# The opening layer norm split anew between ScalarE and VectorE, and sixteen one-column products moved ahead of the first q matmul

## The chip, the cores and the metric

One core of one Trainium2 chip. The metric is device time in microseconds (us) of one execution. "PE" is TensorE's matmuls, "PEld" its weight loads, "DVE" VectorE, "ACT" ScalarE, "POOL" GpSimd, "SP" the engine that issues nearly all DMAs. Executions of the same program on the same chip spread by about 1 us here (0.1%), which is more than the whole effect that this change aims at. A load "lands" when its last packet has arrived; a "slot" is the time from the start of one matmul to the start of the next.

## The reference, cut to what matters

```python
mod = silu(c) @ w_mod                  # six vectors of 1024: shift sa, scale ca, ...
h   = layernorm(x) * (1 + ca) + sa     # x: 2048 x 1024
x   = x + ga * linear_attention(h, wqkv, wo)      # q = h @ wqkv[:, :1024], ...
h   = layernorm(x) * (1 + cb) + sb
x   = x + gb * (silu(h @ w_gate) * (h @ w_up)) @ w_down
```

Only the first norm of the first 512 rows (row tiles 0 to 3), the scale `ca`, the shift `sa` and the first q matmuls matter here.

Of the kernel before, what the change touches and what calls it, by code (L numbers as in the profile page):

```python
# [8 lines left out]
ACT = mybir.ActivationFunctionType  # L9
ALU = mybir.AluOpType  # L10
# [252 lines left out]
def bass_adaLN_cond__linear_attn_block__swiglu_ffn__prompt_kernel(  # L263
# [20 lines left out]
    EPS = 1e-5  # L284

    with ExitStack() as es:
# [14 lines left out]
        XRES = T("xres", 0, [128, NST, D], BF16)  # L301
        PQT = T("pqt", 32 * KB, [128, NHG, S], BF16)
        WCA = T("wca", 32 * KB, [128, NDT, D], BF16)
# [12 lines left out]
        MV = T("mv", SM + 1632, [128, NST, 2], FP32)  # L316
        VE = T("ve", SM + 1760, [128, NST], FP32)
        RSTD = T("rstd", SM + 1824, [128, NST], FP32)
        NEGHALF = T("neghalf", SM + 1888, [128, 4], FP32)
        SUMX = T("sumx", SM + 1920, [128, NST], FP32)  # L320
        SUMSQ = T("sumsq", SM + 1984, [128, NST], FP32)
# [11 lines left out]
        NMR = T("nmr", SM + 2944, [128, NST], FP32)  # L333
# [119 lines left out]
        def warm(n=1, bank=2):  # L453
            for _ in range(n):
                P.pe("matmul", out=PS[:, bank, :], lhsT=IDENT[:], rhs=E1[:, 0, :], start=True, stop=True)
# [6 lines left out]
        def ln1_stats_ops(st):  # L462
            par, j = (st // 4) % 2, st % 4
            return [
                lambda: P.dve("bn_stats", out=STATS[:, par, j, 0, :], in_=XRES[:, st, 0:512]),
                lambda: P.dve("bn_stats", out=STATS[:, par, j, 1, :], in_=XRES[:, st, 512:1024]),
                lambda: P.dve("bn_aggr", out=MV[:, st, :], in_=STATS[:, par, j, :, :]),
            ]
# [10 lines left out]
        def ln1_xn(st):  # L479
            P.dve("tensor_scalar", out=XRES[:, st, :], in0=XRES[:, st, :],  # L480
                  scalar1=MV[:, st, 0:1], scalar2=RSTD[:, st:st + 1], op0=ALU.subtract, op1=ALU.mult)
# [22 lines left out]
        def mod_sc(w, c0, ms):  # L504
            for m in ms:
                for kt in range(NDT):
                    P.pe("matmul", out=PS[:, 0, c0 + m:c0 + m + 1], lhsT=w[:, kt, m * 128:(m + 1) * 128],
                         rhs=SILUC[:, kt:kt + 1], start=mod_first[0], stop=(kt == NDT - 1), skip_group_check=True)
                    mod_first[0] = False
# [48 lines left out]
        def ln1_rstd1(st):  # L558
            P.dve("tensor_scalar", out=VE[:, st:st + 1], in0=MV[:, st, 1:2], scalar1=EPS, scalar2=None, op0=ALU.add)
            P.pool("tensor_tensor", out=RSTD[:, st:st + 1], in0=VE[:, st:st + 1], in1=NEGHALF[:, 0:1], op=ALU.pow)  # L560

        def ln1_xn_act(st):
            P.dve("tensor_scalar", out=NMR[:, st:st + 1], in0=MV[:, st, 0:1], scalar1=RSTD[:, st:st + 1],
                  scalar2=-1.0, op0=ALU.mult, op1=ALU.mult)
            P.act("activation", out=XRES[:, st, :], in_=XRES[:, st, :],
                  func=ACT.Identity, scale=RSTD[:, st:st + 1], bias=NMR[:, st:st + 1])
# [7 lines left out]
        def act_stats(st, c0=0, mid=None):  # L574
            n = (D - c0) // 512
            junk0 = HT[:, 1, 0:2, :] if st < 8 else JUNK1
            for fn_, sc_, acc_ in ((ACT.Identity, 1.0 / D, SUMX), (ACT.Square, D ** -0.5, SUMSQ)):
                P.act("activation", out=junk0[:, 0:n, :], in_=XRES[:, st, c0:D].rearrange("p (a b) -> p a b", a=n),
                      func=fn_, scale=sc_, accum_out=acc_[:, st:st + 1])
                if mid is not None:  # L580
                    mid()
                    mid = None

        def act_mv_ops(st):
            return [
                lambda: P.dve("tensor_copy", out=MV[:, st, 0:1], in_=SUMX[:, st:st + 1]),
                lambda: P.dve("scalar_tensor_tensor", out=MV[:, st, 1:2], in0=SUMX[:, st:st + 1],
                              scalar=SUMX[:, st:st + 1], in1=SUMSQ[:, st:st + 1], op0=ALU.mult, op1=ALU.subtract),
            ]

        def neg_rstd(st):
            P.dve("tensor_scalar", out=VE[:, st:st + 1], in0=MV[:, st, 1:2], scalar1=-1.0, scalar2=EPS, op0=ALU.mult,
                  op1=ALU.add)
            P.pool("tensor_tensor", out=RSTD[:, st:st + 1], in0=VE[:, st:st + 1], in1=NEGHALF[:, 0:1], op=ALU.pow)

        act_stats(2)
        s0_, s1_, s3_ = ln1_stats_ops(0), ln1_stats_ops(1), ln1_stats_ops(3)
        m2 = act_mv_ops(2)

        def tile_transposes(*js):  # L600
            for dt in range(NDT):
                for j in js:
                    c = (dt % 2) * 512 + j * 128
                    P.pe("transpose", out=PSB[:, 4 + dt // 2, c:c + 128], in_=XRES[:, j, dt * 128:(dt + 1) * 128],
                         identity=IDENT[:])

        warm(13, bank=3)
        s0_[0]()
        s0_[1]()
        s1_[0]()  # L610
        s0_[2]()
        ln1_rstd1(0)
        s1_[1]()
        s1_[2]()
        ln1_rstd1(1)
        ln1_xn(0)
        tile_transposes(0)
        warm(5, bank=3)
        s3_[0]()
        ln1_xn_act(1)  # L620
        tile_transposes(1)
        warm(0, bank=3)
        m2[1]()
        m2[0]()
        neg_rstd(2)
        s3_[1]()
        s3_[2]()
        ln1_rstd1(3)
        ln1_xn(2)
        ln1_xn(3)  # L630
        mod_sc(WCA, 8, range(2))
        fin_ca(0, 2)
        tile_transposes(2, 3)
        h0_first(0, "dve")
        h0_first(1, "dve")
        raw_copy(4, "dve")
# [36 lines left out]
        def q_part(nt, bank, dts):  # L673
            for dt in dts:
                P.pe("matmul", out=PS[:, bank, :], lhsT=WQK[:, dt, nt * 128:(nt + 1) * 128],
                     rhs=HT[:, 0, dt, :], start=(dt == 0), stop=(dt == 7))
# [55 lines left out]

        def q_phase_chunk0(side):
            qb = [1, 2, 3, 4, 6, 7, 5]
            for nt in range(4):
                q_part(nt, qb[nt], (0,))
            mod_sc(WCA, 8, range(2, 4))
            fin_ca(2, 2)
            for dt in (2, 3):
                h0_first(dt, "dve")  # L740
            for nts, dts in (((4, 5), (0,)), (range(6), (1,)), ((6,), (0, 1))):
                for nt in nts:
                    q_part(nt, qb[nt], dts)
            mod_sc(WCA, 8, range(4, 8))
            fin_ca(4, 4)
            for dt in (4, 5):
                h0_scale_only(dt)
            for nt in range(7):
                q_part(nt, qb[nt], (2, 3))
            act_stats(4)  # L750
            for nt in range(7):
                if nt == 4:
                    mod_sc(WSA, 0, range(6, 8))
                    fin_sa(6, 2)
                    for dt in (6, 7):
                        h0_scale(dt)
                q_part(nt, qb[nt], (4, 5))
            mod_sc(WSA, 0, range(4, 6))
            fin_sa(4, 2, True)
            for nt in range(7):  # L760
                if nt == 2:
                    bias_mm((4, 5))
                q_part(nt, qb[nt], (6,))
            for nt in range(7):
                if nt == 1:
                    mod_sc(WSA, 0, range(4))
                    fin_sa(0, 4, True)
                    ln_ops[1][0]()
                    ln_ops[1][1]()
                if nt == 4:  # L770
                    bias_mm(range(4))
                    bias_fin()
                q_part(nt, qb[nt], (7,))
            ln_ops[1][2]()
            ln1_rstd1(5)
            for f in act_mv_ops(4):
                f()
            neg_rstd(4)
            q_phi = lambda nt: phi_evac(qb[nt] if nt < 7 else 0, PQT[:, nt, 0:512], bias=BIASQ[:, nt:nt + 1])
            for i, dt in enumerate((4, 5, 0, 1, 2, 3, 6, 7)):  # L780
                P.pe("matmul", out=PS[:, 0, :], lhsT=WQK[:, dt, 896:1024], rhs=HT[:, 0, dt, :], start=(i == 0),
                     stop=(i == 7))
            for dt in (4, 5):
                h0_shift(dt)
            ln1_xn(5)
            th_dma(5)
            for dt in range(4):
                h0_shift(dt)
            ln1_xn(4)
            th_dma(4)  # L790
            for nt in range(8):
                q_phi(nt)
                for f in side.get(nt, []):
                    f()
            qk_ctr[0] = 0
# [401 lines left out]
```

## The kernel before: the parts that the change and the argument touch

The kernel records every operation with its engine; the order of the calls is the order on each engine, and semaphores are added from the data that each one reads and writes. All records therefore carry one line (L176), and the reader goes by the tiles' names: `xres` the rows of x, `stats` and `mv` their statistics, `rstd` 1/sigma, `wca` and `wsa` the weights of scale and shift, `ht` the scaled, transposed rows, `wqk` the weights of q.

```python
P.dma("c", CS8[0:NDT, :], cv8, queue="act")
for st in range(4):
    P.dma("x0_%d" % st, XRES[:, st, :], xv[:, st, :])      # row tiles 0..3
ca_load(0); wq_load(0, 2); ca_load(1); wq_load(2, 2); wq_load(4, 2)
sa_load(1); wq_load(6); wq_load(7); sa_load(0)             # all on one queue
# ... cut ...
def act_stats(st, ...):      # ScalarE: sum of x and sum of x*x, two passes over a tile
def ln1_stats_ops(st):       # VectorE: bn_stats on each half, then bn_aggr
def ln1_rstd1(st):           # VectorE: var + eps;  POOL: pow(-0.5)
# ... cut ...
act_stats(2)                                   # ScalarE sums row tile 2
s0_, s1_, s3_ = ln1_stats_ops(0), ln1_stats_ops(1), ln1_stats_ops(3)
warm(13, bank=3)                               # matmuls that warm TensorE up
s0_[0](); s0_[1](); s1_[0](); s0_[2]()
ln1_rstd1(0)
s1_[1](); s1_[2]()
ln1_rstd1(1)
ln1_xn(0)                                      # VectorE normalises tile 0
tile_transposes(0)
warm(5, bank=3)
s3_[0]()
ln1_xn_act(1)                                  # ScalarE normalises tile 1
tile_transposes(1)
m2[1](); m2[0](); neg_rstd(2)                  # waits for ScalarE's sums of tile 2
s3_[1](); s3_[2]()
ln1_rstd1(3)
ln1_xn(2); ln1_xn(3)
mod_sc(WCA, 8, range(2))                       # scale columns 0-255: 16 one-column products
fin_ca(0, 2)
tile_transposes(2, 3)
h0_first(0, "dve"); h0_first(1, "dve")         # scale columns 0-255 of the transposed tiles
# ... cut ...
def q_phase_chunk0(side):
    for nt in range(4):
        q_part(nt, qb[nt], (0,))               # the first four q matmuls
    mod_sc(WCA, 8, range(2, 4))                # scale columns 256-511
    fin_ca(2, 2)
    # ... cut: the other q matmuls, and among them the products of
    # scale columns 512-1023 and, later, of shift columns 768-1023, 512-767, 0-511
```

## Time and profile before

| | |
|---|---|
| time before | 831.41 us median of 3 (831.29 to 831.42) |
| span of the profiled execution | 829.34 us |
| PE busy | 823.3 us, 99% of the span |
| tile 2 has landed | 5.88 us |
| tile 3's normalise starts | 10.60 us |
| first q matmul | 12.29 us |
| last weight load of the matmul stream | 826.80 us |

The chain that ended last, followed back from the last instruction; columns are start in us, length in us, engine:

```profile
1.71 4.17 DMA xres<-in_A_x_dram
...
5.90 1.16 ACT ht L176 x2
...
7.08 0.88 ACT ht L176
...
12.29 814.80 PE ps L176 x4016
```

It reads: tile 2's load, ScalarE's two sums of it (`ht` is only where their unused output goes), a few small steps of VectorE and POOL, and from 12.29 us one unbroken piece of PE to the end. Whatever starts that piece earlier, or takes work out of it, should shorten the kernel.

The timeline of VectorE in the opening (start, length, engine, operation, tiles; in brackets the idle time before it and what ended that):

```profile
7.09 0.69 DVE L176 BATCH_NORM_STATS2 stats<-xres 128x6 f32<-128x512 bf16 x1
...
8.26 0.22 DVE L176 SCALAR_TENSOR_TENSOR mv<-sumx,sumsq 128x1 f32<-128x1 f32 x1 [0.38 <-ACT ht L176]
...
8.59 0.69 DVE L176 BATCH_NORM_STATS2 stats<-xres 128x6 f32<-128x512 bf16 x1
9.31 0.21 DVE L176 BATCH_NORM_AGGREGATE mv<-stats 128x2 f32<-128x12 f32 x1
...
10.60 0.55 DVE L176 TENSOR_SCALAR xres<-xres,mv,rstd 128x1024 bf16<-128x1024 bf16 x1 [0.44 <-POOL rstd L176]
```

VectorE stands idle for 0.38 us until ScalarE has summed tile 2, and only then goes on to tile 3's second half. The last line is tile 3's normalise. And TensorE's timeline around the first q matmul:

```profile
10.28 0.22 PE L176 MATMUL ps<-ident,xres 128*128 128x128 bf16 x1
11.20 1.01 PE L176 MATMUL ps<-ident,xres 128*128 128x128 bf16 x15 [0.71 <-DVE xres L176]
12.29 1.02 PE L176 MATMUL ps<-ht,wqk 128*128 128x512 bf16 x4
13.15 0.54 PE L176 MATMUL ps<-siluc,wca 128*128 128x1 bf16 x16
13.56 0.38 PE L176 MATMUL ps<-ht,wqk 128*128 128x512 bf16 x1
```

The last of the 15 transposes starts at 12.00 us and takes a slot of 0.056 us, so PE has nothing to do from 12.05 to 12.29 while VectorE scales the first tile; the sixteen products of scale columns 256-511 then stand in q's way for 0.40 us (13.15 to 13.55).

### The profile page before, as it was taken

To read this page: it belongs to the slowest core of one execution; us is meant where nothing else is said; L and a number is where in the kernel's file an instruction comes from. 1 tells how busy PE (TensorE), PEld (TensorE's weight loads), DVE (VectorE), ACT (ScalarE), POOL (GpSimd) and SP (SyncE) were. 2 spreads that over 40 slices of the span, in tenths; PEclk is the share of its full clock that TensorE was granted. 3 is DMA by queue.
4 is the path that set the end of the run, shared out by engine and by line. 5 is a ranking of instruction groups with operands and counts; after the bars stand their busy time and mean duration, and the time that the engine had idled before them with its cause. 6 is when DMAs were issued, how large, how long until landed. Compare 5 with 4: busy or idle time off the path is not lost.

```text
span 829.3 us, 10017 instructions
## 1 busy us (share of the span) xinstructions
PE 823.3 (99%) x4083; PEld 378.8 (46%) x4083; DVE 312.9 (38%) x666; ACT 196.3 (24%) x335; POOL 40.5 (5%) x58
## 2 busy tenths in 40 slices
PE   8999999999999999999999999999999999999998
PEld 4544444454444444444444444444444444444444
DVE  5797986756955521121221111122111211221111
ACT  3658641323232111111111111111110111111011
POOL 1010000000130000030000003000000300000000
DMA  9969655938297986700455571045557004553000
GB/s 320 284 152 229 150 162 172 197 107 304 57 256 226 262 256 184 194 25 13 123 152 153 152 188 34 13 124 154 152 153 193 27 13 124 151 154 91 0 26 26
DMA packets 199246, 119.29 MB, mean 144 GB/s; under 512 B 57880, under 2 KB 182944, under 8 KB 199200
## 3 DMA queue, kind: packets, MB, share of 16 engines
q1 hardware_dynamic: 199184, 118.65, 53.0%
q8 instruction: 32, 0.52, 0.3%
q14 instruction: 14, 0.11, 0.0%
q10 hardware_dynamic: 16, 0.00, 0.0%
HBM read 100.67 MB, written 4.33 MB: 127 GB/s over the span
## 4 chain that ended last, share of the span: by engine, by line
PE 98%; DMA 1%; DVE 0%; ACT 0%; SPq 0%; POOL 0%; issue 0%
PE ps L176 98%; DMA xres<-in_A_x_dram 1%; ACT ht L176 0%; DVE xres L176 0%; SPq L176 0%; POOL rstd L176 0%; DVE stats L176 0%; DVE mv L176 0%; DVE ve L176 0%
## 5 line engine op out<-in xcount | busy, mean ns | idle before, releaser
L176 PE MATMUL ps<-h2t,gug 128*128 128x512 bf16 x896 | 211.7, 379 | 0.0
L176 PE MATMUL ps<-h2t,guu 128*128 128x512 bf16 x896 | 211.7, 379 | 0.0
L176 DVE TENSOR_TENSOR at<-sg,ps 128x512 bf16<-128x512 bf16 x112 | 77.0, 687 | 282.8 <-PE ps L176 281.2
L176 ACT ACTIVATE sg<-ps 128x512 bf16<-128x512 f32 x112 | 66.9, 597 | 309.7 <-PE ps L176 309.7
L176 PEld LDWEIGHTS ps<-h2t,guu 128*128 128x128 bf16 x896 | 87.7, 98 | 105.7
L176 PEld LDWEIGHTS ps<-h2t,gug 128*128 128x128 bf16 x896 | 87.6, 98 | 105.5
L176 PE MATMUL ps<-wd_a,at 128*128 128x512 bf16 (+1 forms) x512 | 112.4, 377 | 0.0
L176 PE MATMUL ps<-ht,wqk 128*128 128x512 bf16 x512 | 111.8, 379 | 0.1
L176 PE MATMUL ps<-wd_b,at 128*128 128x512 bf16 (+1 forms) x384 | 85.0, 377 | 0.0
L176 PEld LDWEIGHTS ps<-wd_a,at 128*128 128x128 bf16 x512 | 50.1, 98 | 59.7
L176 DVE TENSOR_TENSOR ut<-att,gb_b 128x512 bf16<-128x512 bf16 (+1 forms) x32 | 14.1, 441 | 167.0 <-ACT att L176 167.0
L176 PEld LDWEIGHTS ps<-ht,wqk 128*128 128x128 bf16 x512 | 49.4, 98 | 58.7 <-issue 0.2
L176 ACT ACTIVATE att<-ps 128x512 bf16<-128x512 f32 (+1 forms) x32 | 17.4, 591 | 182.1 <-PE ps L176 182.1
L176 PEld LDWEIGHTS ps<-wd_b,at 128*128 128x128 bf16 x384 | 37.6, 98 | 44.7
L176 PE MATMUL ps<-pk,xres 128*128 128x512 bf16 x256 | 56.5, 379 | 0.0
L176 PE MATMUL ps<-mw,pqt 128*128 128x512 bf16 x256 | 56.3, 379 | 0.0
L176 POOL TENSOR_SCALAR h2t<-h2t,modcol 128x512 bf16<-128x512 bf16 x32 | 26.3, 836 | 383.4 <-DMA h2t<-xn 383.4
L176 ACT ACTIVATE e<-ps 128x512 bf16<-128x512 f32 x56 | 33.1, 603 | 31.8 <-PE ps L176 21.3
L176 PEld LDWEIGHTS ps<-mw,pqt 128*128 128x128 bf16 x256 | 24.8, 98 | 30.2 <-DVE xres L176 0.4
L176 PEld LDWEIGHTS ps<-pk,xres 128*128 128x128 bf16 x256 | 24.8, 98 | 30.0 <-issue 0.4
L176 ACT ACTIVATE junk<-xres 128x1024 bf16<-128x1024 bf16 x24 | 25.4, 1058 | 35.1 <-DVE xres L176 34.9
L176 DVE SCALAR_TENSOR_TENSOR xres<-ps,xres 128x512 bf16<-128x512 f32 x32 | 21.4, 688 | 12.3 <-PE ps L176 11.5
(106 smaller groups left out, 345.1 us busy)
## 6 DMA issues: line engine op xcount, KB each, us to landing
gug<-in_B_w_gate_dram SPq DMA_DIRECT2D x56, 512.0 KB, 3.9
guu<-in_B_w_up_dram SPq DMA_DIRECT2D x56, 512.0 KB, 5.2
xres<-in_A_x_dram SPq DMA_DIRECT2D x20, 256.0 KB, 8.0
rb<-recip_den SPq DMA_DIRECT2D x8, 512.0 KB, 11.5
stgx<-in_w_mod_dram SPq DMA_DIRECT2D x2, 2048.0 KB, 7.8
wd_a<-in_B_w_down_dram SPq DMA_DIRECT2D x4, 1024.0 KB, 8.0
out_dram<-xres SPq DMA_DIRECT2D x31, 128.0 KB, 1.7
xres<-in_A_x_dram SPq DMA_DIRECT2D x3, 1024.0 KB, 14.2
```

What stands on the lines that cost most here:

```text
L176: return getattr(e, method)(**kw)
```

## The change

The intent: tile 1 lands before tile 2, so let ScalarE sum tile 1 and normalise tiles 0 and 1, and leave the statistics of the others to VectorE, so that nobody waits for sums of a late tile. And multiply scale columns 256-511 in PE's wait ahead of q.

```diff
-        act_stats(2)
-        s0_, s1_, s3_ = ln1_stats_ops(0), ln1_stats_ops(1), ln1_stats_ops(3)
-        m2 = act_mv_ops(2)
+        s0_, s2_, s3_ = ln1_stats_ops(0), ln1_stats_ops(2), ln1_stats_ops(3)
+        # act_var(st): VectorE, variance of a tile that ScalarE summed
+        # act_xn(st, mean): VectorE, -mean*rstd; ScalarE, the normalise
         warm(13, bank=3)
-        s0_[0](); s0_[1](); s1_[0](); s0_[2]()
+        act_stats(1)
+        s0_[0](); s0_[1](); s0_[2]()
         ln1_rstd1(0)
-        s1_[1](); s1_[2]()
-        ln1_rstd1(1)
-        ln1_xn(0)
+        s2_[0]()
+        act_xn(0, MV[:, 0, 0:1])
+        s2_[1]()
         tile_transposes(0)
         warm(5, bank=3)
+        act_var(1)
+        s2_[2]()
+        # VectorE: var + eps of tile 2; POOL: one pow for tiles 1 and 2
         s3_[0]()
-        ln1_xn_act(1)
-        tile_transposes(1)
-        m2[1](); m2[0](); neg_rstd(2)
         s3_[1]()
+        act_xn(1, SUMX[:, 1:2])
         s3_[2]()
         ln1_rstd1(3)
         ln1_xn(2)
+        tile_transposes(2)
+        mod_sc(WCA, 8, range(2))
         ln1_xn(3)
-        mod_sc(WCA, 8, range(2))
         fin_ca(0, 2)
-        tile_transposes(2, 3)
+        tile_transposes(1, 3)
+        mod_sc(WCA, 8, range(2, 4))
 ...
-            for nt in range(4):
-                q_part(nt, qb[nt], (0,))
-            mod_sc(WCA, 8, range(2, 4))
             fin_ca(2, 2)
-            for nts, dts in (((4, 5), (0,)), (range(6), (1,)), ((6,), (0, 1))):
+            for nts, dts in ((range(4), (0,)), (range(4), (1,)), ((4, 5, 6), (0, 1))):
```

(Statements are put on one line, comments stand for two short helpers and for one pair of statements, and a `warm(0)`, which does nothing, is left out.) Two pows of POOL became one.

More of the change, by code (lines that the diff above doesn't have):

```diff
@@ L594, in neg_rstd, with act_var, act_xn @@
             P.pool("tensor_tensor", out=RSTD[:, st:st + 1], in0=VE[:, st:st + 1], in1=NEGHALF[:, 0:1], op=ALU.pow)
-        act_stats(2)
-        s0_, s1_, s3_ = ln1_stats_ops(0), ln1_stats_ops(1), ln1_stats_ops(3)
-        m2 = act_mv_ops(2)
+        s0_, s2_, s3_ = ln1_stats_ops(0), ln1_stats_ops(2), ln1_stats_ops(3)
+        def act_var(st):
+            P.dve("scalar_tensor_tensor", out=MV[:, st, 1:2], in0=SUMX[:, st:st + 1], scalar=SUMX[:, st:st + 1],
+                  in1=SUMSQ[:, st:st + 1], op0=ALU.mult, op1=ALU.subtract)
+            P.dve("tensor_scalar", out=VE[:, st:st + 1], in0=MV[:, st, 1:2], scalar1=-1.0, scalar2=EPS, op0=ALU.mult,
+                  op1=ALU.add)
+        def act_xn(st, mean):
+            P.dve("tensor_scalar", out=NMR[:, st:st + 1], in0=mean, scalar1=RSTD[:, st:st + 1],
+                  scalar2=-1.0, op0=ALU.mult, op1=ALU.mult)
+            P.act("activation", out=XRES[:, st, :], in_=XRES[:, st, :],
+                  func=ACT.Identity, scale=RSTD[:, st:st + 1], bias=NMR[:, st:st + 1])
         def tile_transposes(*js):
@@ L607, in bass_adaLN_cond__linear_attn_block__swiglu_ffn__prompt_kernel @@
         warm(13, bank=3)
-        s0_[0]()
-        s0_[1]()
-        s1_[0]()
-        s0_[2]()
+        act_stats(1)
+        for f in s0_:
+            f()
         ln1_rstd1(0)
-        s1_[1]()
-        s1_[2]()
-        ln1_rstd1(1)
-        ln1_xn(0)
+        s2_[0]()
+        act_xn(0, MV[:, 0, 0:1])
+        s2_[1]()
         tile_transposes(0)
         warm(5, bank=3)
+        act_var(1)
+        s2_[2]()
+        P.dve("tensor_scalar", out=VE[:, 2:3], in0=MV[:, 2, 1:2], scalar1=EPS, scalar2=None, op0=ALU.add)
+        P.pool("tensor_tensor", out=RSTD[:, 1:3], in0=VE[:, 1:3], in1=NEGHALF[:, 0:2], op=ALU.pow)
         s3_[0]()
-        ln1_xn_act(1)
-        tile_transposes(1)
-        warm(0, bank=3)
-        m2[1]()
-        m2[0]()
-        neg_rstd(2)
         s3_[1]()
+        act_xn(1, SUMX[:, 1:2])
         s3_[2]()
```

## The prediction

> **What bounds the kernel.** TensorE. The page has PE busy 823.3 of 829.3 us. In the chain that ended last, one unbroken PE piece of 814.8 us starts at 12.29 us, the first q matmul, and runs to the last evacuation; the start-to-start times in the timeline show no gap over 0.3 us after it. So the change can win or lose only by moving 12.29, by taking PE slots out of what follows, or by opening a wait there. The diff removes no matmul: after 12.29 there are the same products less 16 one-column ones (scale columns 256-511), which move ahead of it.
>
> **Before 12.29** (chain of waits, timeline): row tile 2 lands at 5.87; ScalarE sums it (two passes, 2.34 us to the second sum); VectorE, idle 0.38 us, waits for that, computes the variance 8.26-8.67, then second-half statistics of tile 3 at 8.59, aggregate 9.31, pow on POOL 9.78-10.56, normalise 10.60-11.14, 15 transposes from 11.20, first scaled tile at 11.66-12.14, q at 12.29.
>
> **What the change does there.** Tile 1 lands at 4.24, 1.6 us before tile 2, so ScalarE starts its sums earlier and has them at about 6.6 instead of 8.23. VectorE takes tile 2 when it lands. With the trace's start-to-start times (statistics 0.60, aggregate 0.72 after its statistics, dependent small op 0.24, POOL 0.23 after its input and 0.55 to 0.80 long):
> - tile 2 statistics 5.89 and 6.57 (small negative-mean op between), tile 1's variance 7.2-7.4 with no wait for ScalarE, tile 2's aggregate 7.5, epsilon 7.7, one pow for both 8.0-8.7;
> - tile 3 statistics 7.8 and 8.4, aggregate 9.1, epsilon 9.36, pow 9.6-10.4, normalise 10.4-10.95.
> So tile 3's normalise starts about 0.2 us earlier (10.4 against 10.60). VectorE gives up a 1024-wide normalise (0.54) for four small ops and loses its 0.38 wait. ScalarE's two normalises (1.23 each) at about 6.7 and 9.2 end by 10.45, before they are needed at about 10.9. Estimates, all worked out from this trace.
>
> **The moved 16 products.** Each takes a 25 ns slot, 0.404 us in all (13.150 to 13.554). The Trainium skill, "TensorE: Matmul & The Clock Gate", section "Wait — 56ns, not 53.3ns?", gives about 25 ns as the floor between small matmuls; this trace agrees. Between the last transpose's slot (12.05) and q (12.29) PE has 0.24 us free while VectorE scales the first tile. In the new place 0.24 of the 0.404 is hidden; q itself then starts 0.16 later than without them.
>
> **Sum.** 0.2 (norm) + 0.24 (hidden products) = about 0.4 us. A cap: the shift columns 512-1023 land at 20.79 and are used at 21.26, columns 0-511 land at 25.16 and are used at 25.59; DMA times don't move, so gains beyond about 0.43 us would turn into PE waits there. Predicted 831.03 us, -0.05%; 830.2 to 831.8. Within 2%: 0.98; faster 0.01; slower 0.01.
>
> **Checks.** q's first matmul at about 12.25 (0.03 earlier) though the 16 products precede it; no products between the first q matmuls; tile 3's pow at about 9.6; PE gap before the 16 products at 56 ns, not 240; the PE piece after q shorter by 0.4; PE gaps at 20.8 and 25.2 under 0.1 us.
>
> **What would make it wrong.** Tile 2 or 3 landing later (run jitter); the two-column pow taking over 1 us, which delays ScalarE's second normalise; the later first transposes (8.0 instead of 7.23) leaving PE idle 0.9 us so that its clock drops (the same page says a full idle window of about 3.4 us is needed, so I don't expect it): then q's matmuls would start 0.43 us apart instead of 0.216 and 1 to 2 us would be lost.

## The result, and the profile after

831.32 us median of 6 (830.77 to 831.68), against 831.41 for the kernel before in the same rounds (6 runs, 830.98 to 831.49). The ratio is 0.9999, with a 95% interval from 0.9986 to 1.0012: the same. A ratio here is the mean time of one kernel's fast runs over that of the other's of the same rounds, so it is not quite the ratio of the medians. Executions over 1.5% slower than the fastest of the same kernel are left out of the means.

The forecast of 831.03 with 830.2 to 831.8 holds the time. But the 0.4 us that it counted on are not to be seen in the totals: the means differ by 0.06 us.

A caution on the traces. All of them but the first of the kernel before lack 78 of the 4083 matmul records, one in every 50 from q on, and so the chain of waits is cut into hundreds of pieces; the one of after starts its q matmuls at 12.20 only because the first one's record is missing. The weight loads are complete, so times of the stream are read from those.

VectorE's timeline after, answering to the one above:

```profile
5.33 0.69 DVE L176 BATCH_NORM_STATS2 stats<-xres 128x6 f32<-128x512 bf16 x1
6.18 0.21 DVE L176 TENSOR_SCALAR nmr<-mv,rstd 128x1 f32<-128x1 f32 x1 [0.16 <-POOL rstd L176]
6.31 0.68 DVE L176 BATCH_NORM_STATS2 stats<-xres 128x6 f32<-128x512 bf16 x1
6.91 0.20 DVE L176 SCALAR_TENSOR_TENSOR mv<-sumx,sumsq 128x1 f32<-128x1 f32 x1
...
7.52 1.28 DVE L176 BATCH_NORM_STATS2 stats<-xres 128x6 f32<-128x512 bf16 x2
...
10.13 0.55 DVE L176 TENSOR_SCALAR xres<-xres,mv,rstd 128x1024 bf16<-128x1024 bf16 x1 [0.45 <-POOL rstd L176]
```

The wait for ScalarE's sums is gone (6.91 has no bracket), and tile 3's normalise starts at 10.13 instead of 10.60. TensorE after, matmuls and then weight loads:

```profile
10.60 1.15 PE L176 MATMUL ps<-ident,xres 128*128 128x128 bf16 x16
11.58 0.54 PE L176 MATMUL ps<-siluc,wca 128*128 128x1 bf16 x16
```

```profile
11.81 0.22 PEld L176 LDWEIGHTS ps<-siluc,wca 128*128 128x128 bf16 x6
11.96 0.98 PEld L176 LDWEIGHTS ps<-ht,wqk 128*128 128x128 bf16 x6
...
824.48 1.71 PEld L176 LDWEIGHTS ps<-wdg,at 128*128 128x128 bf16 x28
```

The weight loads before, for comparison:

```profile
12.26 0.56 PEld L176 LDWEIGHTS ps<-ht,wqk 128*128 128x128 bf16 x4 [0.22 <-issue]
...
825.19 1.71 PEld L176 LDWEIGHTS ps<-wdg,at 128*128 128x128 bf16 x28
```

The products follow the transposes at once, and q's first weights follow the products with no hole: 11.96 against 12.26 us in the trace of before, with the products already behind it. From scale columns 512-1023 to the very end the weight loads stand 0.71 us earlier than before (four single ones apart); the last one is at 826.09 instead of 826.80. So in this trace the matmul stream gained 0.71 us, nearly twice the forecast. The span, however, is 828.99 against 829.34: only 0.36 us shorter. The rest went after the last DMA. POOL's two closing semaphore steps are not in the views of the profile, but in the trace's records; the last steps of the other engines wait for the second of them:

| trace | last output DMA issued | POOL's last step but one | POOL's last step | between | end of span |
|---|---|---|---|---|---|
| before | 827.43 | 829.155 | 829.240 | 0.085 | 829.34 |
| after | 826.72 | 828.45 | 828.884 | 0.435 | 828.99 |

Two questions follow. Is the 0.35 us at the end chance or part of the change? And is the 0.71 us a property of the change or of this trace, where tile 2 landed at 4.96 instead of 5.88 us?

### The profile page after: what moved, and what is told of

Its sections match the earlier page's. It is cut to its first block, busy times and chain, and to the rows that moved or that the text cites. A ratio compares the mean times of both kernels' runs of the same rounds, so it can differ in the third digit from the quotient of the medians.

```text
span 829.0 us, 9939 instructions
## 1 busy us (share of the span) xinstructions
PE 819.6 (99%) x4005; PEld 379.2 (46%) x4083; DVE 312.5 (38%) x665; ACT 197.5 (24%) x336; POOL 40.4 (5%) x57
## 4 chain that ended last, share of the span: by engine, by line
PE 97%; DVE 2%; issue 1%; ACT 0%; DVEq 0%; ACTq 0%
PE ps L176 97%; DVE acc L176 1%; DVE pkt L176 0%; DVE e L176 0%; DVE pqt L176 0%; DVE ht L176 0%; DVE mask L176 0%; ACT e L176 0%; DVE xres L176 0%; DVE zsel L176 0%; DVE modcol L176 0%; DVEq L247 0%; ACTq L247 0%
```

## The experiments

My theory: the norm and the moved products each gain what I counted at equal landings; what is gained is taken back, partly by the closing step of POOL, which is longer because POOL's program has one instruction fewer, partly by waits for loads whose landings don't move with the stream. The rivals: the landing is all there is to the gain; the products, or the norm, give all or nothing; the long end is jitter. Twelve kernels in three calls, each call on one chip with 9 runs of the kernel before. Each of the twelve ran five times. The totals (means, us; "fewer/as many" is POOL's program against that of before):

| run | POOL program | mean | mean of before | ratio, 95% interval |
|---|---|---|---|---|
| before_again | as many | 831.30 | 831.00 | 1.0004 (0.9991 to 1.0016) |
| after_again | one fewer | 831.39 | 831.00 | 1.0005 (0.9992 to 1.0017) |
| products_only | as many | 831.01 | 831.00 | 1.0001 (0.9987 to 1.0014) |
| norm_only | one fewer | 831.37 | 831.00 | 1.0005 (0.9992 to 1.0017) |
| after_pad | as many | 830.88 | 831.12 | 0.9998 (0.9986 to 1.0011) |
| before_less | one fewer | 831.63 | 831.12 | 1.0007 (0.9995 to 1.0020) |
| after_pad_slack | as many | 830.83 | 831.12 | 0.9999 (0.9985 to 1.0012) |
| early_slack | as many | 831.27 | 831.12 | 1.0003 (0.9990 to 1.0016) |
| after_third | one fewer | 831.52 (4 fast runs) | 831.32 | 1.0002 (0.9989 to 1.0016) |
| after_pad_slack5 | as many | 831.13 | 831.32 | 0.9997 (0.9983 to 1.0010) |
| after_pad_slack5_x1act | as many | 831.58 | 831.32 | 1.0003 (0.9991 to 1.0016) |
| after_pad_x3first | as many | 831.61 | 831.32 | 1.0004 (0.9991 to 1.0016) |

No interval excludes 1, and the control, the kernel before against itself, reads 1.0004. Totals can't carry the argument. The traces can (times in us from the span's start; "stream" is the first weight load of q, "end of stream" the last weight load of all):

| trace | tile 2 landed | tile 3 normalised | stream | shift columns 512-1023 landed | end of stream | POOL's last two steps apart |
|---|---|---|---|---|---|---|
| before | 5.88 | 10.60 | 12.26 | 20.79 | 826.80 | 0.085 |
| before_again | 5.53 | 10.26 | 12.19 | 20.68 | 826.73 | 0.080 |
| products_only | 5.83 | 10.54 | 12.38 | 20.93 | 826.56 | 0.085 |
| early_slack | 5.86 | 10.58 | 12.54 | 21.06 | 827.25 | 0.080 |
| before_less | 5.68 | 10.40 | 12.36 | 20.82 | 827.05 | 0.414 |
| norm_only | 5.93 | 10.51 | 12.17 | 21.32 | 827.16 | 0.410 |
| after | 4.96 | 10.13 | 11.96 | 20.40 | 826.09 | 0.435 |
| after_again | 5.68 | 10.26 | 12.09 | 20.87 | 826.52 | 0.414 |
| after_pad | 5.52 | 10.14 | 11.97 | 21.26 | 826.89 | 0.080 |
| after_pad_slack | 5.50 | 10.07 | 11.90 | 20.31 | 826.23 | 0.085 |
| after_pad_slack5 | 6.37 | 10.94 | 12.77 | 20.28 | 827.16 | 0.085 |
| after_pad_x3first | 7.29 | 11.86 | 13.69 | 20.30 | 827.82 | 0.085 |
| after_pad_slack5_x1act | 4.23 | 10.53 | 12.36 | 21.32 | 827.72 | 0.080 |

(The profile of after_third, in which TensorE was granted 0.949 of its clock, is left out of the table.)

### before_again: the control

Edit: none.

> The kernel before, unchanged, as a control for jitter. My theory says the total carries two things that no kernel here controls: when row tile 2 lands (5.87 us in the first trace of before, 4.97 in the first trace of after) and the last semaphore step of POOL (0.085 us in one trace, 0.435 in the other). Expected: total 831.4 within 0.5; if tile 2 lands at about 5.0 here, the first q matmul comes 0.0 to 0.4 us before 12.29, because tile 2 is on the chain through ScalarE's sums; if it lands at 5.9, q at 12.29 within 0.1. Rival (the landing does not matter, the norm's own work bounds it): q at 12.29 within 0.1 whatever the landing.

Tile 2 landed at 5.53, 0.35 us sooner than in the first trace, and tile 3's normalise came 0.34 us sooner. That is the chain of the theory. q, however, came only 0.07 us sooner, because another load stood in the way; the weight loads of this trace:

```profile
10.67 0.46 PEld L176 LDWEIGHTS ps<-siluc,wca 128*128 128x128 bf16 x16 [1.02 <-DMA wca<-in_w_mod_dram]
11.06 0.29 PEld L176 LDWEIGHTS ps<-ident,xres 128*128 128x128 bf16 x5
```

Here the weights of scale columns 0-511 landed at 10.62 (9.62 in the first trace), and the products of columns 0-255 stand ahead of the last transposes. So the opening has two gates, tile 2 and the scale weights, and which one closes last differs between executions. (By q alone the rival would stand: 0.07 us is within its 0.1. It is tile 3's normalise that speaks against it, and after_pad_x3first below.) The scale weights landed late, at 10.58 to 10.80 us, in three of the five traces with the old norm and in none with the new one (at most 10.32), so what a late landing costs the changed kernel is not shown.

### after_again: the changed kernel again

Edit: none against the changed kernel.

> The changed kernel again, as a control. My theory: first q weight load at 11.97 us if tile 2 lands near 5.0, at about 12.25 if it lands near 5.9; the stretch from q's start to the last evacuation 0.40 us shorter than in before in either case. Total 0.4 to 0.7 us below the kernel before on the mean, blurred by 0.35 us of the last semaphore step. Rival (all of the gain is luck of the landing): with tile 2 at about the same time as in the control of before, the matmul stream comes at the same time as there.

q's weights at 12.09, 0.10 us before those of the control, with the products behind them: the stream up to the shift columns is 0.50 us earlier than in before_again. It doesn't last:

```profile
20.92 0.47 PEld L176 LDWEIGHTS ps<-siluc,wsa 128*128 128x128 bf16 x16 [0.57 <-DMA wsa<-in_w_mod_dram]
...
25.29 0.87 PEld L176 LDWEIGHTS ps<-siluc,wsa 128*128 128x128 bf16 x32 [0.37 <-DMA wsa<-in_w_mod_dram]
```

The weight loads of the shift products wait for their DMA. (The bracket is PEld's idle time; since it runs ahead of PE, PE itself lost less, and the start-to-start times of the weight loads show 0.25 us lost at the first and 0.05 at the second.) In the first trace of before the same loads had no wait:

```profile
21.05 0.67 PEld L176 LDWEIGHTS ps<-siluc,wsa 128*128 128x128 bf16 x16
...
25.38 1.06 PEld L176 LDWEIGHTS ps<-siluc,wsa 128*128 128x128 bf16 x32
```

At the end of the stream 0.21 us are left, and POOL's end takes 0.33. The span is 829.38, against 829.27 in the control. I had expected the total to fall by 0.4 to 0.7 us and the stretch from q to the end to be 0.40 us shorter than in before; the total did not fall, and the stretch was 814.43 us against 814.54, so 0.11 shorter: a miss. Both takers are of the theory, but I had not expected so much of the first.

### products_only and norm_only: one half each

Edit of products_only (on the kernel before):

```diff
         tile_transposes(2, 3)
+        mod_sc(WCA, 8, range(2, 4))
 ...
-            for nt in range(4):
-                q_part(nt, qb[nt], (0,))
-            mod_sc(WCA, 8, range(2, 4))
             fin_ca(2, 2)
-            for nts, dts in (((4, 5), (0,)), (range(6), (1,)), ((6,), (0, 1))):
+            for nts, dts in ((range(4), (0,)), (range(4), (1,)), ((4, 5, 6), (0, 1))):
```

> The kernel before with the 16 one-column products alone moved (the old norm kept). My theory: they fill the 0.24 us in which PE waits for the first scaled tile and push q 0.16 us back, so q at 12.45 us where tile 2 lands at 5.87, and the common matmul stream (everything after scale columns 512-1023) 0.24 us earlier than before; total -0.24. Rival A (the products give the whole gain, because they leave the q stream): stream 0.40 us earlier, q still at 12.29. Rival B (the products only change place): stream unchanged.

Weight loads of this trace:

```profile
11.94 0.51 PEld L176 LDWEIGHTS ps<-siluc,wca 128*128 128x128 bf16 x16
12.38 0.55 PEld L176 LDWEIGHTS ps<-ht,wqk 128*128 128x128 bf16 x4
```

Tile 3's normalise was 0.06 us earlier than in before (landing); q's weights came 0.12 later, so 0.17 later by the products (0.16 expected); the stream behind scale columns 512-1023 was 0.29 earlier, 0.23 without the landing (0.24 expected). Both rivals fall: the products neither give 0.40 nor merely change place. 0.05 us were lost again at shift columns 0-511.

Edit of norm_only: the changed kernel with the products in their old place (the last hunk of the change undone, and the line `mod_sc(WCA, 8, range(2, 4))` behind the transposes taken out).

> The changed norm with the products left in their old place after the first four q matmuls. My theory: tile 3's normalise starts 0.2 us earlier where tile 2 lands at 5.9 and 0.45 us earlier where it lands at 5.0; q and the whole stream move by the same; so stream -0.2 to -0.47, and a 0.24 us hole ahead of q again. Rival (the norm split gives nothing, VectorE bound as before): tile 3's normalise at 10.6 and stream unchanged at equal landing.

At a landing of 5.93, tile 3's normalise at 10.51. The hole ahead of q is back (weight loads):

```profile
12.17 0.56 PEld L176 LDWEIGHTS ps<-ht,wqk 128*128 128x128 bf16 x4 [0.22 <-issue]
```

Set beside the other traces, this makes a rule. In the five traces with the old norm, tile 3's normalise starts 4.72 to 4.73 us after tile 2's landing. In six traces with the new norm (norm_only, after_again, after_pad, the two slack kernels, after_pad_x3first) it starts 4.57 to 4.62 us after it. So at equal landing the new norm is worth 0.14 us, not 0.2. In the first trace of after (landing 4.96) it started at 10.13, as in after_pad (landing 5.52, 10.14): below about 5.5 VectorE is still busy with tile 0 (in that trace its step for tile 0 at 6.18 waits for POOL's `rstd`), and an earlier landing gains nothing.

In norm_only the stream then lost what it had: the shift columns landed at 21.32, as late as in any trace, and at 45 us it waited again and lost 0.20 us, for tiles of the next chunk, which VectorE could scale only when a transfer (`ht<-xres`) had landed:

```profile
44.91 0.10 PEld L176 LDWEIGHTS ps<-ht,wqk 128*128 128x128 bf16 x1 [0.20 <-DVE ht L176]
```

### after_pad and before_less: POOL's last step

Edit of after_pad, on the changed kernel:

```diff
         P.pool("memset", ap=NEGHALF[:], constant=-0.5)
+        P.pool("memset", ap=NEGHALF[:], constant=-0.5)
```

> The changed kernel plus one POOL instruction that does nothing new (a second fill of the constant -0.5 at the start, when POOL is idle), so that POOL's program has as many instructions as before. Theory: the change removes one pow from POOL, and that shifts a page boundary of POOL's instruction stream between its last two semaphore steps, which then lie 0.41 to 0.44 us apart in after, after_again and norm_only, against 0.080 to 0.085 us in before, before_again and products_only; with the extra instruction they are 0.08 us apart again, an 8192-byte instruction fetch stands near 651 us and none after the end of the span, and the total is 0.34 us below that of the changed kernel (about 830.9 where that has 831.2). Rival 1 (the end depends on how the matmul stream ends, or is jitter): 0.41 to 0.44 us as in after_again. Rival 2 (it depends on ScalarE's or VectorE's changed instruction count): 0.41 to 0.44 us as well.

Edit of before_less, on the kernel before:

```diff
-        add(s1, 7, lambda: P.pool("memset", ap=ZHL[:], constant=0.0))
+        add(s1, 7, lambda: P.dve("memset", ap=ZHL[:], constant=0.0))
```

> The kernel before with one POOL instruction fewer: the clearing of one small tile in the middle of the program is given to VectorE. Nothing of the change is in it. Theory (POOL's instruction count sets where the page boundary falls): the last two semaphore steps of POOL lie 0.41 to 0.44 us apart, the matmul stream is where it is in before, the total is 0.34 us above the kernel before. Rival (the changed norm or the stream's timing makes the end longer): 0.08 us apart and the total unchanged.

As to POOL's step, both came out as the theory says. With the superfluous instruction the last two steps are 0.080 us apart; with one instruction fewer in the kernel before, which has nothing of the change, 0.414 us. Over all 14 traces, the five with one POOL instruction fewer show 0.410 to 0.435 us and the nine others 0.080 to 0.085, whatever the norm, the stream or the other engines' counts. The page of the profile has a trace of it too, in the list of DMA queues (packets, MB, share), for the instruction fetches that fall within the span; before, after, after_pad and before_less in that order:

```profile
q14 instruction: 14, 0.11, 0.0%
```

```profile
q14 instruction: 13, 0.11, 0.0%
```

```profile
q14 instruction: 14, 0.11, 0.0%
```

```profile
q14 instruction: 13, 0.11, 0.0%
```

In the packets' records, an 8192-byte fetch stands at 651.4 us in before and at 651.3 in after_pad, 1.1 to 1.2 us after POOL's last computing instruction, when POOL has only the end left to wait for. With one instruction fewer this fetch is gone from there and one stands 0.6 to 0.9 us after the end of the span instead (829.85 in after, 830.50 in before_less). The Trainium skill, "Runtime: NRT & Kernel Launch", section "Instruction fetch mechanics", says that a sequencer fetches its next block while it executes the current one and that crossing a boundary is mostly hidden. This fits a boundary that lies between POOL's last two steps when its program is one instruction shorter. That the count of instructions sets the step is shown, for these two counts and with the instruction taken out or put in at different places. That a boundary is what takes the 0.33 us is only inferred from the moved fetch. This fetch itself starts 0.7 to 1.0 us after POOL's last step (828.88 in after, 829.81 in before_less), so it is not what the step waits for; at most it marks the place.

The rest of what I expected of before_less missed. Its stream is not where it is in before: q's weights came 0.10 us later, behind scale weights that landed at 10.80, and 0.15 us more were lost at 45 us, as in norm_only, so it ended 0.25 us later. Its mean total, 0.51 us above the kernel before instead of 0.34, is inside the noise.

The total of after_pad, 0.24 us below that of before on the mean, has the expected sign and is inside the noise. The trace of after_pad is a plain case of the other taker: its stream was 0.70 us earlier than before's when it came to the shift columns, and these landed at 21.26:

```profile
21.30 0.47 PEld L176 LDWEIGHTS ps<-siluc,wsa 128*128 128x128 bf16 x16 [1.07 <-DMA wsa<-in_w_mod_dram]
```

From there on it was 0.06 us later than before, and 0.09 at the end. One late load took the whole gain.

### after_pad_slack and after_pad_slack5: more room for the shift columns

Edit of after_pad_slack, on after_pad (after_pad_slack5 has 5 in place of the first 6):

```diff
-                if nt == 4:
+                if nt == 6:
                     mod_sc(WSA, 0, range(6, 8))     # shift columns 768-1023
 ...
-                if nt == 1:
+                if nt == 3:
                     mod_sc(WSA, 0, range(4))        # shift columns 0-511
 ...
-                if nt == 4:
+                if nt == 6:
                     bias_mm(range(4))
```

> The changed kernel with the POOL instruction restored, and with two groups of one-column products put later among the q matmuls of chunk 0: those of shift columns 768-1023 by two q groups (0.86 us) and those of shift columns 0-511 with their bias products by two q matmuls (0.43 us), so that their weights, which landed between 20.40 and 21.32 us and between 24.77 and 25.68 us in the six traces so far, are there when PE comes to them. Theory (the landings of the shift columns took 0.25 and 0.05 us of the stream's gain in after_again): no PE wait for them, the stream 0.55 to 0.75 us earlier than in before from the q groups to its end, total 0.5 to 0.7 us below the kernel before. Rival (PE is not held by these loads, the loss lies in q's later stages): as after_pad.

> As after_pad_slack, but the products of shift columns 768-1023 only one q group later than in the change (0.43 us) instead of two: with two, VectorE's tile of the later scale was not ready for the next q group, and PE waited 0.2 us for it (in early_slack twice 0.3). Theory: no such wait now; with the shift columns landing at 21.0 or before there is no wait for them either; stream 0.6 to 0.75 us before that of the first trace of before; mean total 0.4 to 0.6 us below the kernel before. Rival (that wait has another cause): PE waits 0.2 us for the scaled tile as before, stream -0.57.

In both, no weight load waited for `wsa`. after_pad_slack has the shortest span of all, 828.77, with the stream 0.77 us earlier than before's at first and 0.57 at the end; its total, 0.29 us below the kernel before on the mean, falls short of the 0.5 to 0.7 expected and is inside the noise. I put the missing 0.2 us down to this line of its matmuls, a wait for the tile that the late shift products belong to, and built after_pad_slack5 to be rid of it:

```profile
22.91 0.38 PE L176 MATMUL ps<-ht,wqk 128*128 128x512 bf16 x1 [0.18 <-DVE ht L176]
```

That reading was wrong. In after_pad_slack5 the wait is gone and the 0.2 us are lost all the same (stream 0.10 later than before's at first, 0.30 later after the bias products). From the last shift product ahead of this place to the first bias product behind it, both traces take 0.55 us: the wait only used time that is otherwise spent waiting for the bias products' input. The loss lies further on. The result of the bias products must be copied out of a bank of PSUM, the memory that matmuls write to, before the last q group can use that bank. With these products moved from ahead of the fifth of seven matmuls to ahead of the seventh (`nt` counts from 0), one matmul instead of three is left to cover the copy. The weight loads behind it, of after_pad_slack and of after_pad_slack5:

```profile
27.90 3.14 PEld L176 LDWEIGHTS ps<-ht,wqk 128*128 128x128 bf16 x16 [0.32 <-DVE biasq L176]
```

```profile
28.77 2.27 PEld L176 LDWEIGHTS ps<-ht,wqk 128*128 128x128 bf16 x12 [0.32 <-DVE biasq L176]
```

The matmuls on the two sides of it start 0.40 us apart in both, instead of 0.216. So the slack bought freedom from the loads (after_pad's 0.79 us) and cost 0.2. As tile 2 landed at 6.37 in the trace of after_pad_slack5, its stream started late (12.77) and, after 0.06 us more were lost at 146 us, ended at 827.16; expected was 0.6 to 0.75 us ahead of before's: a miss. Its total, 0.19 us under the kernel before, shows nothing either.

### early_slack: the products in another gap, with the old norm

Edit, on products_only with the later shift products of after_pad_slack:

```diff
-        mod_sc(WCA, 8, range(2))
+        mod_sc(WCA, 8, range(4))
         fin_ca(0, 2)
         tile_transposes(2, 3)
-        mod_sc(WCA, 8, range(2, 4))
```

> The old norm; the 16 products of scale columns 256-511 put right behind those of columns 0-255, in PE's 0.87 us wait for tile 3's normalise, instead of behind the transposes; and the same two groups of shift products later as in after_pad_slack. POOL's program is that of before. Theory: the products are wholly hidden (0.40 us, not 0.24), q starts at the old 12.2 to 12.3, the stream is 0.40 us earlier, the end is 0.08 us; total 0.4 us below the kernel before, so better than the whole change (0.0) with no change to the norm. Rival A (moved products don't count, only the norm does): total as before. Rival B (they delay the transposes of tiles 2 and 3): tile 3's transposes start later than 11.2.

A miss, in the way of rival B. In the first trace of before there were 0.87 us free at this place. Here the scale weights landed at 10.58, and all 32 products stood behind that landing and ahead of the transposes:

```profile
10.63 0.95 PE L176 MATMUL ps<-siluc,wca 128*128 128x1 bf16 x32 [0.47 <-DMA wca<-in_w_mod_dram]
11.44 1.05 PE L176 MATMUL ps<-ident,xres 128*128 128x128 bf16 x16
```

Tile 3's normalise ended at 11.13, the transposes started at 11.44, q's weights came at 12.54. (The same 0.2 us behind the bias products, 0.10 us at 45 us and 0.27 us at 146 us were lost later.) A gap that one trace shows is no gap if the load that closes it moves by 1 us between executions. In the change's own place the sixteen moved products stand behind the transposes and can't hold these up; those of columns 0-255 still stand ahead of the transposes of tiles 1 and 3.

### after_pad_x3first: tile 2 late on purpose

Edit, on after_pad:

```diff
-        for st in range(4):
+        for st in (0, 1, 3, 2):
             P.dma("x0_%d" % st, XRES[:, st, :], xv[:, st, :])
```

> The changed kernel with the POOL instruction restored and tiles 2 and 3 loaded in the other order, so tile 2 lands where tile 3 did, at 6.2 to 6.8 us instead of 5.0 to 5.9. Theory (tile 2's landing starts VectorE's chain tile 2 statistics to tile 3's normalise): that chain starts 0.9 to 1.3 us later, tile 3's normalise at 10.9 to 11.4 and the first q matmul at 12.7 to 13.2 instead of 12.0; the products still end without a hole ahead of q; the shift columns are then no longer waited for; total 0.5 to 0.9 us above after_pad. Rival (ScalarE's sums or the scale columns' landing bound the opening): q at 12.0 to 12.3 as in after_pad.

Tile 2 landed at 7.29, VectorE waited for it:

```profile
7.31 0.69 DVE L176 BATCH_NORM_STATS2 stats<-xres 128x6 f32<-128x512 bf16 x1 [1.97 <-DMA xres<-in_A_x_dram]
```

Against after_pad the landing is 1.77 us later, tile 3's normalise 1.72, q's first weights 1.72. So tile 2's landing passes to q almost one for one. (The landing was later than I had expected, hence also q at 13.69 instead of 12.7 to 13.2.) After q nothing was lost: the stream from q to the end took 814.13 us, the value that the change should give (814.54 in before, less 0.41 for the products). The total of this run is 0.73 us above that of after_pad, but the two ran on different chips; against the kernel before of each the difference is 0.53. Both figures are inside the noise. In the traces, the 1.72 us at q's start are 0.93 at the end of the stream, because after_pad lost its 0.79 at the shift columns: part of an early start is lost later, in the kernels that have one.

### after_pad_slack5_x1act: tile 1 on another queue

Edit, on after_pad_slack5:

```diff
-            P.dma("x0_%d" % st, XRES[:, st, :], xv[:, st, :])
+            P.dma("x0_%d" % st, XRES[:, st, :], xv[:, st, :], queue="act" if st == 1 else "sp")
```

> As after_pad_slack5, with row tile 1 loaded from ScalarE's queue instead of the common one, so that the loads behind it are issued one issue (0.43 us) earlier. Theory (issue time of the queue sets the landings of the first tiles): tile 2 lands 0.2 to 0.45 us earlier, near 5.2, the scale and shift columns up to 0.4 us earlier; tile 3's normalise at 9.9 or before, stream another 0.1 to 0.3 us earlier. Rival (landings are set by the transfer rate, not by the issue): landings and stream as in after_pad_slack5 within their jitter of 0.5 us; ScalarE's first activation delayed by 0.4 us costs nothing in either case.

Tile 2 landed at 4.23, earlier still than expected (near 5.2). But tile 1 was now issued behind it (1.40 us against 1.24 in the trace's records) and landed at 4.91 (4.13 to 4.52 in the other traces): the two had changed places, and the changed norm hangs on ScalarE's sums of tile 1:

```profile
7.29 0.22 DVE L176 SCALAR_TENSOR_TENSOR mv<-sumx,sumsq 128x1 f32<-128x1 f32 x1 [0.41 <-ACT ht L176]
```

Tile 3's normalise at 10.53. The wait that the change had taken out with tile 2 is back with tile 1. The later loads did not land earlier than in the other traces (scale columns 0-511 at 9.69, elsewhere 9.38 to 10.80; the shift columns at 21.32). The Trainium skill, "DMA: Bandwidth & Descriptors", section "Issuing engines are not separate DMA queues", says that DMAs from several engines run on the same 16 DMA engines and that issuing from more than one saves only the issue time; the later loads of this run agree. It also lost 0.15 us at 45 us and 0.76 us at 146 us, where PE waited for VectorE's `g`, which waited for a small tensor's way through memory; a fourth place where a DMA, not the stream, sets the time.

### after_third

Edit: none against the changed kernel.

> The changed kernel a third time, to stand on the same chip beside its mended versions. Expected by the theory of the POOL page: last semaphore steps 0.41 to 0.44 us apart, instruction fetch after the end of the span; mean total 0.34 us above that of the two mended versions' common part, so 0.0 to 0.4 us above the kernel before. Rival (the long end is chance): 0.08 us.

Four fast runs, mean 831.52, 0.20 us above the kernel before; the profile fell in the slow state, so only its closing step is noted: 0.410 us. Over the first rounds and these two calls, the changed kernel was 0.06 us below, 0.39 above and 0.20 above the kernel before, each inside the noise.

## Why the prediction was right or wrong

**The time: right**, within the range, and "within 2%" was never in doubt for a change that touches the first 12 of 829 us. The hit proves little: the time of the kernel before, 831.41, lies in the range as well.

**What bounds the kernel: right in the main.** From q on PE runs to the end. But the page's PE piece "to the last evacuation" hides that its start is not the only thing that sets it. Transfers with landings of their own stand in it at 20.9, 25.3, 45 and 146 us, and in the first trace of before the stream lost nothing at them.

**The norm, 0.2 us: right in kind, mis-sized.** Tile 3's normalise comes 4.57 to 4.62 us after tile 2's landing instead of 4.71 to 4.73, so 0.14 us. The prediction's "10.4" at a landing of 5.87 would have been 10.45. The 0.47 us of the first pair of traces was mostly the landing.

**The moved products, 0.24 us: right.** 0.23 us measured with the products alone; q 0.17 us later by them (0.16 predicted); no hole left ahead of q. The Trainium skill, "TensorE: Matmul & The Clock Gate", section "Wait — 56ns, not 53.3ns?", gives the floor of about 25 ns that the prediction used, and these traces show it as well: 16 products in 0.404 us.

**Both together, 0.4 us: right where the stream begins.** In five traces with the whole change and tile 2 landing at 5.50 or later (after_again, after_pad, the two slack kernels, after_pad_x3first), the q weight loads behind scale columns 256-511, corrected for the difference of tile 2's landing, are 0.34 to 0.39 us earlier than in the first trace of before. Set against the two traces of the old kernel with late scale weights, the gain would look larger; that part goes with the landing of the scale weights and is not shown to be of the change.

**The cap, "gains beyond about 0.43 us would turn into PE waits": right in kind, mis-sized.** The step that failed is "DMA times don't move". The landing of shift columns 512-1023 moved between 20.28 and 21.32 us in the fast traces, of tile 2 (in the old order of loads) between 4.96 and 6.37. In after_again the cap took 0.30 us, in after_pad 0.79, in the first trace of after nothing. The gain is not 0.4 us with a cap at 0.43, but somewhere between about 0 and 0.4, decided by the landings of each execution. The prediction had looked at two of the places where the stream meets transfers; at the others, kernels with the old norm and with the new one lost 0.10 to 0.20 us (at 45 us, in four traces) and 0.06 to 0.76 us (at 146 us, in three).

**The term that was missing:** +0.33 us at the end, from a POOL program that is one instruction shorter. I had read "one pow for both" as a saving of VectorE's and POOL's time, and not looked at what the count does to POOL's instruction stream.

The sum, at an equal landing of tile 2: -0.14 (norm) -0.23 (products) + 0 to 0.79 (shift columns) + 0.33 (POOL's end), so about 0 where the loads are in time and a loss where they are late; losses at 45 and 146 us, which kernels of both sorts have, come on top. This is what the totals show, as far as they show anything.

**The fear of a colder clock: not borne out.** q's matmuls ran 0.216 us apart from the first. The warm-up matmuls were 0.427 us apart until 5.57 us in before and until 7.70 in after, but this varies with the execution and not with the kernel (6.00 in after_again, 7.52 in products_only). In after_pad_x3first 1.83 us passed between the last of the first 13 warm-up matmuls and the first transpose behind it, and the warm-up matmuls that followed ran 0.216 us apart all the same. The Trainium skill, "TensorE: Matmul & The Clock Gate", section "Part 1: The HAM clock gate", calls the window free-running and the turn run-variable; the traces agree that the turn varies.

What stays open: whether the changed kernel with POOL's instruction put back is truly faster than the kernel before. Three versions of it read 0.24, 0.29 and 0.19 us below, and the two with other loads of the row tiles 0.29 and 0.26 us above; each interval spans about 2 us. What takes the 0.33 us in POOL's last step is open too. The best guess for a version that keeps the gain (after_pad_slack5 with the bias products ahead of an earlier matmul than the seventh) was not run.

## What to carry to other kernels

A gain of a few tenths of a microsecond at the head of a long stream arrives at its end only if every load that the stream meets later has more room than that; look for such loads' landings in several traces, not in one, because one trace shows only one of the landings that occur. Before a rearrangement is judged by the span, compare start times of the same instruction in both traces, from the opening to the last one, and the few steps behind the last one too: a shift that stays constant and then vanishes names the place that took it. And a step that costs 0.33 us only because an unrelated engine has one instruction fewer is undone with one instruction that does nothing.

## What the Trainium skill lacked or had wrong

- "Runtime: NRT & Kernel Launch", section "Instruction fetch mechanics": it calls the crossing of an instruction block mostly hidden and names 16 KiB blocks. Here POOL's program, one instruction shorter, has 0.41 to 0.435 us between its last two steps instead of 0.08, in five traces of five, and the packet that moved with it is 8192 bytes. If a block boundary is the cause, which is inferred and not shown, it is not hidden there; the page says nothing of a boundary at the end of a program.
- "DMA: Bandwidth & Descriptors": nothing on how much the landing of the same load moves between executions of the same program. Here: 1.4 us for the third load of the kernel (4.96 to 6.37), 1.0 us for 1 MB some 20 us into it (20.28 to 21.32).
- "Perfetto Trace Analysis": nothing on missing matmul records. Here 78 of 4083 are missing, one in every 50 from q on, in all traces but one, with all weight loads there; a gap of two slots (0.43 us) in the matmuls is then no idle time.
